# Weight combinations on VectorE in the gaps of tile 0, value copies in two halves, transposes one block later

## Chip, cores, metric

One core of a Trainium2 chip. The metric is the device time of one execution in microseconds (us), the median of several runs; before the change 313.4 us (lowest 312.9, highest 314.9). A "span" is the time from the first to the last instruction in a trace; it is some 1.7 us shorter than the device time of the same run.

## The reference, cut to what matters

```python
# attention: q, k, v of (batch 8, heads 8, seq 576, head_dim 64), window 32
scores = (q @ k.T) / 8                        # only where |i - j| <= 32
attn   = softmax(scores)                      # per row
x      = (attn @ v)  as  (4608 tokens, 512)
# feed-forward: w_in (512, 2048), w_out (2048, 512)
out    = gelu_tanh(x @ w_in) @ w_out          # float32 out
```

## The kernel before

The feed-forward runs over nine tiles (0 to 8) of 512 tokens. While TensorE multiplies tile t with `w_out`, the attention of batch t+1 is woven in between. From tile 1 on the second product is a Winograd-like scheme with 7 products in place of 8, which needs sums of activations (S1..S4, made per tile on VectorE) and combinations of weights made once: T1 = B12 - B11, T2 = B22 - T1, T3 = B22 - B12, T4 = B21 - T2, each 128 x 2048 in fp16 from quarters B of `w_out`.

For batch 2 and later, q and k are cast to fp16 on VectorE and transposed by DMA (`QT`, `KT`); the scores of tile t need `KT` of batch t+1. The values go straight into `V` by DMA from GpSimd's queue, and `pair_v` copies half of them to other partitions.

```python
PLAN_0 = {0: "s1@1 w0 w1", 4: "m0 m1", 12: "w2", ..., 52: "v2@0 v3@1",   # what is done at which step of tile 0
          56: "x2 t4", 57: "c1", 60: "x3", 64: "s4@1 m4"}                # s scores, m mask, v weigh, x spread,
...                                                                      # w cast w_out, t tails, c combine
def combine(i, eng):
    dst, x, y = wino["todo"][i]
    eng.tensor_tensor(dst, x, y, op=ALU.subtract)
...
                elif kind == "c":            # step 57 of tile 0
                    combine_w()
                    combine(1, nc.gpsimd)    # T1
...
        if t == 0:                           # after tile 0's last step
            for t4, yo in later:
                store(0, t4, yo)
            combine(2, nc.gpsimd)            # T2
            load_table(gelu_set)
...
def cast_and_turn(b):                        # first thing of tile 1 on VectorE (cut)
    queries(qr, q16, 0, 128)                 # 4 casts of q, then the DMA transpose QT<-q
    for pr in range(NPAIR):
        nc.vector.tensor_copy(k16[:, pr, :, :, :], kr[:, :, 2 * pr:2 * pr + 2, :])
        if pr % 2:
            nc.sync.dma_start_transpose(KT ... <- k16 of pairs pr - 1 and pr)
...
            for fc in range(begun, NF):      # input product of tile 1
                ffn_in(t, fc)
                if t == 1 and fc in (8, 12):
                    combine(fc // 4 + 1, nc.vector)          # T3, T4
                if t == 1 and fc == 3:
                    nc.gpsimd.tensor_copy(after, gTs[1][:, column(1, 2), 0:1])   # wait for the third gelu
                    load_v(2)                                # values of batch 2, from GpSimd's queue
...
            if t == 1 and i == 20:           # behind the masks m0 and m1 of step 16
                pair_v(unpaired.pop(0), nc.vector.tensor_copy)
```

The softmax here doesn't subtract the row's maximum and nothing guards it: scores larger than these inputs give would overflow.

Of the kernel before, what the change touches and what calls it, by code (L numbers as in the profile page):

```python
# [10 lines left out]
FP16 = mybir.dt.float16  # L11
# [25 lines left out]
def cut(b):  # L37
# [11 lines left out]



TURN_0 = {11: 0, 12: 1, 14: 2, 15: 3}
PLAN_0 = {0: "s1@1 w0 w1", 4: "m0 m1", 12: "w2", 18: "s2@0 s-1@1 m-1", 22: "d0", 24: "m2 d1",
          28: "s3@0 v-1@1 x-1", 30: "w3", 31: "m3", 34: "d2", 36: "v0@0 v1@1 x0 d3 x1", 52: "v2@0 v3@1",
          56: "x2 t4", 57: "c1", 60: "x3", 64: "s4@1 m4"}

ORDER_0 = [(t4, 4 * w + i) for w in range(4) for t4 in range(4)
           for i in ((2, 3, 0, 1) if w == 0 else range(4))]
# [6 lines left out]
def kernel(  # L65
# [9 lines left out]
    nc = tc.nc  # L75
# [25 lines left out]
    stage = ctx.enter_context(tc.tile_pool(name="stage", bufs=5))  # L101
# [19 lines left out]
    w_out16 = big.tile([128, NF, DM], FP16, name="w_out16")  # L121
# [50 lines left out]
    def load_v(b):  # L172
        V = Vs[b % 2]
        for c in range(4):
            nc.gpsimd.dma_start(V[:, c, :, :],  # L175
                                v[b, :, 128 * c:128 * c + 128, :].rearrange("h p d -> p h d"))
        nc.gpsimd.dma_start(V[0:64, 7, :, :], v[b, :, 512:S, :].rearrange("h p d -> p h d"))  # L177

    def pair_v(b, copy, hs=slice(0, H)):

        V = Vs[b % 2]
        copy(V[64:128, 4:8, hs, :], V[64:128, 0:4, hs, :])
        copy(V[0:64, 4:7, hs, :], V[0:64, 1:4, hs, :])  # L183
# [4 lines left out]
    def stage_w():  # L188
        return stage.tile([128, 4, 512], FP32, name="wst", tag="stage")
# [5 lines left out]
    def load_w_out(i, w, c0=0, c1=4):  # L195
        nc.sync.dma_start(w[:, c0:c1, :], w_out_v[:, 4 * i + c0:4 * i + c1, :])
        return w

    def cast_w(w, dst, on_dve=2, cs=range(4), on_act=()):
        for c in cs:  # L200
            (nc.scalar.copy if c in on_act else nc.vector.tensor_copy if c < on_dve else nc.gpsimd.tensor_copy)(  # L201
                dst[:, c, :], w[:, c, :])
# [59 lines left out]
    def cast_early(b, pr, engs):  # L262
        for src, dst, eng in zip(raws[b][0:2], halfs[b][0:2], engs):
            eng.tensor_copy(dst[:, pr, :, :, :].rearrange("p j h d -> p h j d"),
                            src[:, 2 * pr:2 * pr + 2, :].rearrange("p h (j d) -> p h j d", j=4))
# [24 lines left out]
    def trans_pair(b, pr, pt, now=True):  # L290
        q16, k16 = halfs[b][0:2]
        for j in range(4):
            nc.tensor.transpose(pt[:, j, :], q16[:, pr, j, :, :], idn)
        for j in range(4):
            nc.tensor.transpose(pt[:, 4 + j, :], k16[:, pr, j, :, :], idn)
        if now:
            trans_out(b, pr, pt)
# [134 lines left out]
    def column(t, n):  # L432

        return n // 2 + 8 * (n % 2) if t else n
# [27 lines left out]
    def gelu(t, n):  # L462
        fc = column(t, n)
        nc.scalar.activation(gTs[t][:, fc, :], phs[fc], AF.Gelu_apprx_tanh)  # L464
        if t and n % 4 == 3:
            sums(t, n // 4)

    wino = {}

    def combine_w():  # L470

        t12 = stage.tile([128, 2, 8, 256], FP16, name="t12", tag="stage")
        t34 = stage.tile([128, 2, 8, 256], FP16, name="t34", tag="stage")
        B11, B12, B21, B22 = (w_out16[:, r:r + 8, c:c + 256] for r in (0, 8) for c in (0, 256))
        T1, T2, T3, T4 = t12[:, 0], t12[:, 1], t34[:, 0], t34[:, 1]
        s12 = stage.tile([128, 2, 8, 256], FP16, name="s12", tag="stage")
        s34 = stage.tile([128, 2, 8, 256], FP16, name="s34", tag="stage")
        yo = stage.tile([128, 4, 512], FP32, name="y4", tag="stage")
        wino.update(B11=B11, B21=B21, B22=B22, T1=T1, T2=T2, T3=T3, T4=T4, S1=s12[:, 0],
                    S2=s12[:, 1], S3=s34[:, 0], S4=s34[:, 1], yo=yo,  # L480
                    todo={1: (T1, B12, B11), 2: (T2, B22, T1), 3: (T3, B22, B12), 4: (T4, B21, T2)})

    def combine(i, eng):
        dst, x, y = wino["todo"][i]
        eng.tensor_tensor(dst, x, y, op=ALU.subtract)  # L485
# [29 lines left out]
    later, unpaired = [], []  # L515
# [97 lines left out]
    wo = [load_w_out(0, stage_w())]  # L613
# [73 lines left out]
    split = (nc.gpsimd, nc.vector)  # L687
    cast_early(1, 0, split)
    cast_early(1, 1, split)
    for fc in range(6, NF):  # L690
        if fc in (11, 12):
            cast_early(1, fc - 9, split)
        if fc in TURN_0:
            pr = TURN_0[fc]
            if pr < 2:
                pt = psS.tile([128, 2, 8, 128], FP16, name="pt", tag=f"S{pr}")
            trans_pair(1, pr, pt[:, pr // 2] if pr < 3 else
                       psO.tile([128, 8, 128], FP16, name="pt", tag="O"))
        ffn_in(0, fc)
# [5 lines left out]
    for t in range(NT):  # L705
        b = t + 1
        att = b < B
        if t:
            for fc in range(begun):
                ffn_in(t, fc, 3, 4, then=False)  # L710
            for fc in range(begun):
                gelu(t, fc)
            if att and b > 1:
                cast_and_turn(b)
            for fc in range(begun, NF):
                ffn_in(t, fc)
                if t == 1 and fc in (8, 12):
                    combine(fc // 4 + 1, nc.vector)
                if t == 1 and fc == 3:

                    nc.gpsimd.tensor_copy(after, gTs[1][:, column(1, 2), 0:1])
                    load_v(2)
                    unpaired.append(2)
        plan = PLAN_0 if not t else PLAN if att else {5: "v-1", 31: "x-1"} if t == B - 1 else {}

        def group(g):
            return (b, g) if g >= 0 else (b - 1, 4)

        if plan and t:
            load_table(exp_set)  # L730
        if t and b + 1 < B:
            load_qk(b + 1)
        ods = {}
        for i in range(113 if t else 65):
            for act in plan.get(i, "").split():
                kind, at = act[0], int(act[act.index("@") + 1:]) if "@" in act else None
                g = int(act[1:].split("@")[0])
                if kind == "w":
                    if g == 3:
                        cast_v(1, 2)  # L740
                    cast_w(wo[g], w_out16[:, 4 * g:4 * g + 4, :], on_act=(1,) if g else ())
                    if g == 2:
                        cast_v(1, 0)
                        cast_v(1, 1)
                    if g == 3:
                        cast_v(1, 3)
                        cast_vt(1)
                        cast_tails(1, nc.gpsimd)
                        load_qk(2)
                elif kind == "t":  # L750
                    trans_tails(1, bank16(1))
                elif kind == "c":
                    combine_w()
                    combine(1, nc.gpsimd)
                elif kind == "s":
                    score(*group(g), at)
                elif kind == "d":
                    pair_v(b, nc.vector.tensor_copy, slice(2 * g, 2 * g + 2))
                elif kind == "m":
                    mask(*group(g))  # L760
                elif kind == "v":
                    bb, gg = group(g)
                    o, d = weigh(bb, gg, at)
                    ods[g] = (o, invert(bb, gg, o, d))
                    if t and g < 0 and b + 1 < B:
                        load_v(b + 1)
                        unpaired.append(b + 1)
                    if t and g == (3 if att else -1):
                        load_table(gelu_set)
                else:  # L770
                    spread(*group(g), *ods[g])
            if t == 1 and i == 20:
                pair_v(unpaired.pop(0), nc.vector.tensor_copy)
            if t == 0 and i in (61, 62):
                store(0, *later.pop(0), eng=nc.scalar)
            if t == 0 and i < 64:
                ffn_out_0(*ORDER_0[i])
            elif t and i < 112:
                ffn_out(t, i)
        if t == 0:  # L780
            for t4, yo in later:
                store(0, t4, yo)
            combine(2, nc.gpsimd)
            load_table(gelu_set)
        else:
            ffn_last(t)
        if unpaired:
            pair_v(unpaired.pop(), nc.sync.dma_start)
        begun = 3 if t < NT - 1 else 0
        for fc in range(begun):  # L790
            ffn_in(t + 1, fc, 0, 3)
# [28 lines left out]
```

## Time and profile before

| | before | what it says |
|---|---|---|
| time, median of runs | 313.4 us | the yardstick |
| the run whose trace was given | 310.07 us, span 308.4 us | faster than each of the timed runs of its session; this will matter |
| start of tile 1 (first L456 matmul after tile 0) | 58.9 us | tile 0 and the first attention |
| tile 1 | 39.4 us | the later tiles take 30.4 us |
| start of tile 2 to the end | 210.1 us | the same in every kernel below but one |

The last row makes the reading simple: span = start of tile 1 + length of tile 1 + 210.1. The lines that this comes from stand in the prediction.

### The profile page before, as it was taken

Reading aid. Unit: us, or ns where it says so; the run is one execution under the profiler, and the core shown is the slowest. Engines: PE = TensorE matmul, PEld = TensorE weight load, DVE = VectorE, ACT = ScalarE, POOL = GpSimd, SP = SyncE. Lnnn points to the kernel's source line nnn. Section 1 sums busy time; section 2 is a strip of 40 time slices with the busy share of each in tenths; the row PEclk is TensorE's granted clock in tenths of the full one; section 3 lists DMA queues with packets and bytes.
Section 4 is the critical chain, followed back from the end, with each engine's and each line's share of the span. In section 5 each row is a group of like instructions: output and inputs, shape, how many; then the busy total and the mean of one; then the engine's idle time right before and its main releaser. Section 6 shows DMA issues by size and latency. Waiting matters only on the chain.

```text
span 308.4 us, 7131 instructions
## 1 busy us (share of the span) xinstructions
PE 289.0 (94%) x2886; PEld 181.2 (59%) x2886; DVE 195.8 (63%) x425; ACT 186.9 (61%) x287; POOL 112.7 (37%) x162
## 2 busy tenths in 40 slices
PE   6989799895789999999999999999999999999993
PEld 2534444442567468746874686468646864784582
DVE  4783559799467846775677577666866644533451
ACT  1567385675355787478747874787478757705600
POOL 3666454896003910390049004800530051016000
PEclk9999999999699999999999999999999999999999
DMA  6999999979995999799979996999592022004013
GB/s 197 256 362 369 376 278 257 244 150 153 158 249 131 175 155 248 177 161 131 255 170 201 182 236 153 186 173 227 128 206 40 2 62 76 3 0 136 2 41 97
DMA packets 116831, 52.44 MB, mean 170 GB/s; under 512 B 97519, under 2 KB 109551, under 8 KB 116798
## 3 DMA queue, kind: packets, MB, share of 16 engines
q1 hardware_dynamic: 84233, 39.66, 59.2%
q0 software_dynamic: 31776, 11.41, 31.3%
q10 hardware_dynamic: 789, 0.92, 0.9%
q8 instruction: 22, 0.36, 0.5%
q14 instruction: 11, 0.09, 0.1%
HBM read 36.70 MB, written 9.44 MB: 150 GB/s over the span
## 4 chain that ended last, share of the span: by engine, by line
PE 77%; DMA 11%; SPq 5%; DVE 3%; POOL 1%; issue 1%; ACT 0%; DVEq 0%
PE mm L547 31%; PE mm L456 18%; PE ph L456 14%; DMA wst<-in_moe_w_in_dram 4%; PE ps_s L360 3%; DMA KT<-k 3%; PE ps_d L389 2%; DMA kr<-in_k_dram 2%; PE mm L521 2%; PE ps_o L395 2%; DMA kt<-in_k_dram 2%; SPq L145 2%; PE py L521 2%; SPq L136 1%; POOL t L485 1%
## 5 line engine op out<-in xcount | busy, mean ns | idle before, releaser
L456 PEld LDWEIGHTS <-w_in 128*128 128x128 f16 x576 | 56.0, 98 | 66.4 <-POOL w_in L201 1.4
L511 POOL DMA_DIRECT2D out_dram<-y x77 | 46.4, 610 | 114.6 <-DVE y L576 100.9
L456 PE MATMUL mm<-xT,w_in 128*128 128x512 f16 x320 | 78.6, 379 | 0.9 <-POOL w_in L201 0.7
L464 ACT ACTIVATE gT<-mm 128x512 f16<-128x512 f32 x80 | 47.6, 599 | 46.4 <-PE mm L456 45.6
L456 PE MATMUL ph<-xT,w_in 128*128 128x512 f16 x256 | 64.1, 379 | 0.0
L495 DVE TENSOR_TENSOR s<-gT 128x512 f16<-128x512 f16 x64 | 26.8, 419 | 41.7 <-ACT gT L464 41.7
L547 PEld LDWEIGHTS <-s 128*128 128x128 f16 x512 | 49.7, 98 | 6.0
L370 ACT ACTIVATE pe<-ps_s 128x960 f16<-128x960 f32 (+1 forms) x32 | 30.5, 976 | 30.6 <-PE ps_s L360 30.6
L547 PE MATMUL mm<-t,s 128*128 128x256 f16 x376 | 44.7, 273 | 0.0
L464 ACT ACTIVATE gT<-ph 128x512 f16<-128x512 f32 x64 | 36.0, 602 | 10.1 <-PE ph L456 9.9
L547 PEld LDWEIGHTS <-gT 128*128 128x128 f16 x384 | 36.6, 99 | 7.1
L547 PE MATMUL mm<-w_out,gT 128*128 128x256 f16 x256 | 34.0, 280 | 0.0
L409 ACT ACTIVATE lt<-lt 128x480 f32<-128x480 f32 (+3 forms) x40 | 23.5, 587 | 1.3
L175 POOL DMA_DIRECT2D V<-in_v_dram x24 | 22.2, 945 | 0.8 <-PE mm L456 0.8
L90 ACT ACT_TABLE_LOAD x17 | 21.8, 1283 | 1.1 <-PEq L804 0.8
L376 DVE TENSOR_TENSOR pe<-pe,band 128x960 f16<-128x960 f16 (+1 forms) x32 | 20.7, 662 | 2.5 <-ACT pe L370 2.5
L408 ACT ACTIVATE lt<-ps_d 128x480 f32<-128x480 f32 (+2 forms) x29 | 16.1, 554 | 10.0 <-PE ps_d L389 6.2
L360 PE MATMUL ps_s<-QT,KT 64*64 64x128 f16 (+3 forms) x576 | 13.6, 221 | 6.3 <-DMA KT<-k 5.6
L395 PEld LDWEIGHTS <-V 128*64 128x64 f16 x520 | 14.5, 112 | 5.9 <-DVE V L183 2.8
L360 PEld LDWEIGHTS <-KT 64*64 64x64 f16 x576 | 10.0, 109 | 13.2 <-DMA KT<-k 6.1
L547 PE MATMUL mm<-t,gT 128*128 128x256 f16 x128 | 16.3, 273 | 0.0
L177 POOL DMA_DIRECT2D V<-in_v_dram x6 | 4.6, 772 | 28.2 <-PE ps_o L395 28.2
(92 smaller groups left out, 324.2 us busy)
## 6 DMA issues: line engine op xcount, KB each, us to landing
kr<-in_k_dram SPq DMA_DIRECT2D x32, 256.0 KB, 8.2
qr<-in_q_dram SPq DMA_DIRECT2D x6, 1024.0 KB, 8.2
wst<-in_moe_w_in_dram SPq DMA_DIRECT2D x3, 1024.0 KB
wst<-in_moe_w_out_dram SPq DMA_DIRECT2D x3, 1024.0 KB, 11.9
V<-in_v_dram POOLq DMA_DIRECT2D x24, 128.0 KB, 8.0
qr<-in_q_dram SPq DMA_DIRECT2D x8, 256.0 KB, 10.7
vr<-in_v_dram SPq DMA_DIRECT2D x16, 128.0 KB, 4.1
V<-V SPq DMA_DIRECT2D x5, 256.0 KB
```

Of the source, the lines that this page charges most:

```text
L90: nc.scalar.add_instruction(mybir.InstLoadActFuncSet(name=nc.get_next_instruction_name(), act_func_set_id=which, ins=[], outs=[]))
L175: nc.gpsimd.dma_start(V[:, c, :, :], v[b, :, 128 * c:128 * c + 128, :].rearrange("h p d -> p h d"))
L360: nc.tensor.matmul(ps[64 * half:64 * half + 64, h, 4 * n * r:4 * n * r + 4 * n].rearrange("k (j p) -> k j p", j=4)[:, :, p0 - q0:p1 - q0], ...
L370: nc.scalar.activation(pe, ps[:, :, 0:w], AF.Exp, scale=SCALE)
L376: nc.vector.tensor_tensor(pe, pe, m.rearrange("k (o j) p -> k o j p", o=1).broadcast_to(list(pe.shape)), op=ALU.mult)
L395: nc.tensor.matmul(o[64 * h:64 * h + 64, cols].rearrange("d (j p) -> d j p", j=4)[:, :, p0 - q0:p1 - q0], Vs[b % 2][:, slot, 2 * pr + h, : ...
L409: nc.scalar.activation(lt[:, 0:n], lt[:, 0:n], AF.Exp, scale=-1.0)
L456: nc.tensor.matmul(ph, w_in16[:, dc, fc * 128:fc * 128 + 128], xT[:, dc, t * 512 % RING:t * 512 % RING + 512], start=(dc == 0), stop=(dc = ...
L464: nc.scalar.activation(gTs[t][:, fc, :], phs[fc], AF.Gelu_apprx_tanh)
L495: nc.vector.tensor_tensor(dst, x, y, op=op)
L511: (eng or turn_about[0] if t == NT - 1 else eng or nc.gpsimd).dma_start(out_v[b, j, q0 + p:q0 + p + e, cols], yo[m:m + e, cols])
L547: nc.tensor.matmul(pys["apart"][:, 0:256] if apart else py[:, blk, :], lhsT, wino[w][:, f, :], start=(new and i % (8 if one else 16) == 0) ...
```

## The change

The intent: take the two combinations T1 and T2 from GpSimd (4.06 and 4.07 us in the trace before) and put them on VectorE, where T3 and T4 take 1.22 us each in that trace, into gaps in which VectorE waited; copy the values of batch 2 in two halves, the first ahead of the masks; transpose batch 1 one block later, so that key casts don't stand ahead of the copies out of PSUM (the buffers in which the kernel puts TensorE's products).

```diff
--- before.py
+++ after.py
@@ -49,10 +49,10 @@
 
 
 
-TURN_0 = {11: 0, 12: 1, 14: 2, 15: 3}
-PLAN_0 = {0: "s1@1 w0 w1", 4: "m0 m1", 12: "w2", 18: "s2@0 s-1@1 m-1", 22: "d0", 24: "m2 d1",
-          28: "s3@0 v-1@1 x-1", 30: "w3", 31: "m3", 34: "d2", 36: "v0@0 v1@1 x0 d3 x1", 52: "v2@0 v3@1",
-          56: "x2 t4", 57: "c1", 60: "x3", 64: "s4@1 m4"}
+TURN_0 = {12: 0, 13: 1, 14: 2, 15: 3}
+PLAN_0 = {0: "s1@1 w1", 4: "m0 m1", 12: "w2", 17: "c1", 18: "s2@0 s-1@1 m-1", 22: "d0", 24: "m2 d1",
+          28: "s3@0 v-1@1 x-1", 30: "w3", 31: "m3", 34: "d2", 36: "v0@0 v1@1 x0 d3 x1", 52: "v2@0 v3@1 c2",
+          56: "x2", 60: "x3 t4", 64: "s4@1 m4"}
 
 ORDER_0 = [(t4, 4 * w + i) for w in range(4) for t4 in range(4)
            for i in ((2, 3, 0, 1) if w == 0 else range(4))]
@@ -468,17 +468,21 @@
     wino = {}
 
     def combine_w():
-
         t12 = stage.tile([128, 2, 8, 256], FP16, name="t12", tag="stage")
+        B11, B12, B21, B22 = (w_out16[:, r:r + 8, c:c + 256] for r in (0, 8) for c in (0, 256))
+        wino.update(B11=B11, B21=B21, B22=B22, T1=t12[:, 0], T2=t12[:, 1],
+                    todo={1: (t12[:, 0], B12, B11), 2: (t12[:, 1], B22, t12[:, 0])})
+        return B12
+
+    def wino_rest(B12):
         t34 = stage.tile([128, 2, 8, 256], FP16, name="t34", tag="stage")
-        B11, B12, B21, B22 = (w_out16[:, r:r + 8, c:c + 256] for r in (0, 8) for c in (0, 256))
-        T1, T2, T3, T4 = t12[:, 0], t12[:, 1], t34[:, 0], t34[:, 1]
+        T3, T4 = t34[:, 0], t34[:, 1]
         s12 = stage.tile([128, 2, 8, 256], FP16, name="s12", tag="stage")
         s34 = stage.tile([128, 2, 8, 256], FP16, name="s34", tag="stage")
         yo = stage.tile([128, 4, 512], FP32, name="y4", tag="stage")
-        wino.update(B11=B11, B21=B21, B22=B22, T1=T1, T2=T2, T3=T3, T4=T4, S1=s12[:, 0],
+        wino.update(T3=T3, T4=T4, S1=s12[:, 0],
                     S2=s12[:, 1], S3=s34[:, 0], S4=s34[:, 1], yo=yo,
-                    todo={1: (T1, B12, B11), 2: (T2, B22, T1), 3: (T3, B22, B12), 4: (T4, B21, T2)})
+                    todo=wino["todo"] | {3: (T3, wino["B22"], B12), 4: (T4, wino["B21"], wino["T2"])})
 
     def combine(i, eng):
         dst, x, y = wino["todo"][i]
@@ -688,10 +692,12 @@
     cast_early(1, 0, split)
     cast_early(1, 1, split)
     for fc in range(6, NF):
-        if fc in (11, 12):
-            cast_early(1, fc - 9, split)
         if fc in TURN_0:
             pr = TURN_0[fc]
+            if pr in (1, 2):
+                cast_early(1, pr + 1, split)
+            if pr == 3:
+                cast_w(wo[0], w_out16[:, 0:4, :])
             if pr < 2:
                 pt = psS.tile([128, 2, 8, 128], FP16, name="pt", tag=f"S{pr}")
             trans_pair(1, pr, pt[:, pr // 2] if pr < 3 else
@@ -750,8 +756,9 @@
                 elif kind == "t":
                     trans_tails(1, bank16(1))
                 elif kind == "c":
-                    combine_w()
-                    combine(1, nc.gpsimd)
+                    if g == 1:
+                        B12 = combine_w()
+                    combine(g, nc.vector)
                 elif kind == "s":
                     score(*group(g), at)
                 elif kind == "d":
@@ -769,8 +776,9 @@
                         load_table(gelu_set)
                 else:
                     spread(*group(g), *ods[g])
-            if t == 1 and i == 20:
-                pair_v(unpaired.pop(0), nc.vector.tensor_copy)
+            if t == 1 and i in (0, 40):
+                pair_v(2, nc.vector.tensor_copy, slice(i // 10, i // 10 + 4))
+                unpaired[:] = [3]
             if t == 0 and i in (61, 62):
                 store(0, *later.pop(0), eng=nc.scalar)
             if t == 0 and i < 64:
@@ -780,7 +788,7 @@
         if t == 0:
             for t4, yo in later:
                 store(0, t4, yo)
-            combine(2, nc.gpsimd)
+            wino_rest(B12)
             load_table(gelu_set)
         else:
             ffn_last(t)
```

## The prediction

"The lock", in it and below, is a name for what the trace before shows: a VectorE operation beside GpSimd's weight combination of 4.07 us ended just after it (a q cast took 4.79 us, 0.415 us in the median of its group). By what means was not tested.

> **What bounds the kernel now.** I first cut the span into tiles with the view of busy time by windows; the edges are the starts of the feed-forward input matmuls (L456) of each tile, taken from the chain that ended last. Columns: window, its length, then busy time of each engine, granted TensorE clock, DMA share, GB/s.
>
> ```profile
> 58.90:98.30 39.40, 32.69 (x343) 21.17 (x332) 30.48 (x55) 23.76 (x35) 15.87 (x16) 0.91 1.25 175
> 98.46:128.87 30.41, 30.41 (x331) 20.01 (x330) 20.89 (x47) 21.55 (x33) 11.39 (x17) 1.00 1.22 187
> 128.87:159.29 30.42, 30.42 (x332) 20.05 (x330) 20.89 (x47) 21.55 (x33) 11.33 (x17) 1.00 1.24 178
> ```
>
> From tile 2 on TensorE is busy all the time and a tile takes 30.4 us; the change touches nothing there. Tile 1 does nearly the same matmuls and takes 98.46 - 58.93 = 39.5 us: **9.1 us too many**. Its clock is also the only one of these at 0.91. That stretch is the prize[...].
>
> Then the chain of waits from tile 0's end into tile 1 (start, length, what held it):
>
> ```profile
> 54.82 4.07 POOL t L485
> ...
> 59.03 5.55 DMA kt<-in_k_dram
> ...
> 65.55 0.75 DVE q L321 x2
> 66.30 2.07 DVE k L329 x4
> 68.37 1.86 DVE qt L321 x4
> 70.23 8.67 DMA KT<-k
> ...
> 78.94 1.01 PE ps_s L360 x30
> ...
> 85.70 0.69 DVE V L182
> 86.40 0.56 DVE V L183
> ```
>
> Tile 1 runs into a wait for the transposed keys of batch 2 (KT), which come through casts on VectorE and DMA transposes, and later into the value copies (L182, L183). The list of waits, filtered for TensorE, gives the sizes:
>
> ```profile
> PE ps_s L360 <- DMA KT<-k: 5.6, 1, 5.6
> PE pt L293 <- DVE KT L301: 1.3, 1, 1.3
> ...
> PE ps_od L395 <- DVE V L183: 1.1, 1, 1.1
> ...
> PE pt L285 <- DVE yo L527: 0.8, 1, 0.8
> ```
>
> The timeline says why KT is late. The casts of q come at 60.41, but:
>
> ```profile
> 60.84 4.79 DVE L321 CAST q<-qr 128x512 f16<-128x512 f32 x1
> 61.27 4.07 POOL L485 TENSOR_TENSOR t<-w_out,t 128x2048 f16<-128x2048 f16 x1
> ```
>
> One cast, 0.415 us in the median of its group, took 4.79 us, and it ends just after GpSimd's 4.07 us weight combination. The two overlap almost exactly: a stand-still of 4.79 - 0.42 = 4.4 us.
>
> Finally the clock, in one-microsecond windows: 1.00 until 76, 0.65 from 76 to 77, 0.50 from 77 to 83, 0.94 from 83 to 84. TensorE went idle at 73.35, so the clock fell after about 3 us of idleness and came back about 4.1 us after work resumed. In those 4.1 us 128x256 matmuls are spaced 2.61 / 12 = 0.217 us, against 3.27 / 29 = 0.113 us later. So about 2.1 us are lost. Check: 5.6 (KT) + 2.1 (clock) + 1.3 (values; 1.1 in the list, 1.4 on the weight-load side) = 9.0 of the 9.1 us.
>
> [...]
>
> **The change part by part.**
>
> *Combination T2 (and T1) from GpSimd to VectorE.* Removed: 2 x 4.06 us on GpSimd, at 54.82 and 61.27. Added: 2 x 1.22 us on VectorE. T1 (step 17) falls into the idle time of 1.37 us before the tail's mask at 45.93; T2 (step 52) into that of 1.19 us before the copy at 55.85. The first gap has GpSimd's casts in it (43.41 to 45.58), so it may stretch by 0.5 us; VectorE is busy 3.90 of 4 us from 46 to 50, so such a delay passes on. After T2 moves, the four q casts take 4 x 0.415 = 1.7 us from about 60.2, so they end near 61.9 in place of 66.3. The DMA transpose of Q is issued near 62 (66.37 before). The loads of k, qt and kt land only by 64.58 (59.03 + 5.55), so k's casts probably wait until about 63.3 (my estimate: the kt load was last in its queue). Two of them, 0.83 us, give 64.2. Q's issue took 3.77 us, so the first K transpose is issued near 65.7 (70.23 before): 4.5 us earlier. With the same 8.67 us, KT lands at 74.4. TensorE reaches the scores near 73.1. **Idle 5.6 becomes about 1.3: -4.3 us.** An idle of 1.3 us did not lower the clock at 35.2, so **-2.1 us** more.
>
> *Value copies in halves.* The 0.69 + 0.55 us before the weighing at 87.01 are replaced by half as much ahead of the masks. TensorE's wait of 1.3 us goes, if the values have landed. Their loads move from 65.62 to about 63.4 (they wait for the third gelu, then GpSimd is free). The fourth is issued near 67; landings run from 4.5 to 10.9 us, so 71.5 to 78. VectorE reaches the first half near 75. If it stands there until 78, masks come late and part of the wait returns: I count **-1.0**.
>
> *Transposes one block later, w0's cast earlier.* The third pair's transposes waited 1.3 us because VectorE held the copies of the second pair behind key casts that waited for DMA. The casts now come after the first pair's copies: locally about -1.1 us. But tile 0 then meets data that comes when it comes: the last value pair lands at 51.9 and x1 ends at 54.06, just before the weighing that needs its bank (54.24). So nearly all of this is taken back. The tail transposes (t4), four steps later, avoid their 0.8 us wait, but T2 now delays the copy of that bank to about 56.6, and the last scores need x3 and the tail copies, near 58.4 instead of 58.63. **-0.3 us** for both.
>
> Sum: 4.3 + 2.1 + 1.0 + 0.3 = 7.7. Since three of the terms can only shrink I take 7.4: 313.68 - 7.4 = **306.3 us**.
>
> **The rivals.** (a) *A DMA bound in place of the lock.* The Q transpose stands behind k's loads in the same queue until 64.6, and the DMA share is 1.9 to 2.0 from 70 to 78. If transposes get going only at 64.6, the 12.5 us from the first Q issue (66.37) to KT (78.9) give 77.1: idle 4.0, clock lost again, and a gain of only 1.5 + 1.0 + 0.3 = 2.8 us (310.9). For it: the queue's order. Against: part of those 12.5 us is Q's issue, which goes on during the loads, and in tiles 2 to 6 KT arrives some 11 us after Q's first issue. I give it 1 in 5. (b) *The values' landing blocks VectorE* ahead of the masks: the 1.3 us stay or grow by 1 us; 307.5 or so. For: landings up to 10.9 us; against: TensorE needs masks only at step 33. (c) *Tile 0 gets longer*, since VectorE is nearly full from 46 to 54: T1 behind GpSimd's casts costs up to 0.5 us; 307. (d) *Everything hides:* no idle at all before the scores and tile 1 at 30.4: gain 9.1 + 0.3, so 304.3.
>
> **Range and chances.** Between (d) at 304.3 and a mix of (b), (c) and a late KT at 309.5 lies most of it; (a) in full is outside. Two per cent is 6.3 us, or 307.4. The base case and (d) clear it, (a) doesn't, (b) and (c) come near it: faster 0.72, same 0.26, slower 0.02; slower would take a new wait larger than the 5.6 us, of which I see no sign.
>
> **What would show it right or wrong.** No GpSimd row L485; four VectorE rows of about 1.22 us; the longest q cast near 0.45 us; the wait of scores for KT at 0 to 2 us; clock 1.00 in tile 1; no wait of L395 for L183 at step 33; tile 1 about 31.5 us instead of 39.5; tile 0's end at 58 to 59. It is wrong if KT lands after 76, if the clock still falls, or if casts of q stand waiting for their load instead of the lock.

## The result, and the profile after

304.1 us in the first session (303.85 to 305.38, 4 runs) against 313.4 us: ratio 0.9704, 95% interval 0.966 to 0.975. A ratio is the mean time of one kernel's fast runs over the mean of the other's fast runs of the same rounds, so not quite the ratio of the medians quoted. Two more sessions on other occasions gave 0.9713 and 0.9764. The time lies 0.2 us below the predicted range of 304.3 to 309.5; the lock was as told, a landing time was not, and the gain was larger: 9.3 us in place of 7.4. (The prediction started from 313.68 us, the median of three runs; the fourth made it 313.4.)

Tile 1 after, by the view of busy time in windows (window, length, busy time of PE, PEld, DVE, ACT, POOL, granted clock, DMA share, GB/s):

```profile
60.69:92.31 31.62, 31.01 (x339) 20.13 (x331) 25.78 (x57) 23.64 (x35) 11.44 (x15) 1.00 1.49 219
```

31.6 us in place of 39.4, at full clock, with 0.6 us idle. (The prediction had said "about 31.5"; its own terms, 39.5 - 4.3 - 2.1 - 1.0, give 32.1.) But the tile starts at 60.7, later than the 58.9 of the trace before. The list of waits of TensorE, with the lines that answer to those of before:

```profile
PE mm L551 <- DVE y L562: 0.5, 1, 0.5
...
PE ps_s L360 <- DVE QT L287: 0.4, 1, 0.4
...
PE pt L293 <- DVE KT L301: 0.2, 1, 0.2
```

The waits for `KT` (5.6) and for the value copies (1.1) are gone; a new one of 0.5 us is for a copy out of PSUM that now stands behind the first half of the value copies, and one of 0.4 us, at the end of tile 0, is for the tails that are transposed later. The wait for L301 went from 1.3 to 0.2, and that for the copy of `yo` (0.8) vanished too.

The timeline of the changed kernel from the casts to the scores (start, length, engine, line):

```profile
62.13 1.43 DVE L321 CAST q<-qr 128x512 f16<-128x512 f32 x4
63.62 3.90 SPq L324 DMA_TRANSPOSE QT<-q  x1
65.24 4.04 POOL L175 DMA_DIRECT2D V<-in_v_dram  x4 [0.35 <-POOL after L727]
65.78 1.97 DVE L329 CAST k<-kr 128x512 f16<-128x512 f32 x4 [2.22 <-DMA kr<-in_k_dram]
67.61 4.25 SPq L331 DMA_TRANSPOSE KT<-k  x2
75.04 0.62 PE L360 MATMUL ps_s<-QT,KT 64*64 64x96 f16 x32
```

Four q casts take 1.43 us, not 5.89. The k casts wait for their load, as predicted. The scores start at 75.04 without a wait for `KT`. The view of DMA issues (last number: us from issue to landing, here of the first of the two `KT` transposes, for which the scores wait) has

```profile
KT<-k SPq DMA_TRANSPOSE x1, 6.0
```

so `KT` landed at 73.6, 6.0 us after its issue at 67.61, not 8.67 (6.5 and 6.9 in the two other sessions' traces). And one more thing has turned round: the Q transpose is now issued 1.6 us ahead of the first value load. Before, the value loads came first:

```profile
65.62 4.28 POOL L175 DMA_DIRECT2D V<-in_v_dram  x4
66.37 3.77 SPq L324 DMA_TRANSPOSE QT<-q  x1
```

### The profile page after: what moved, and what is told of

Same layout as the page of the kernel before. It is cut to its first block, busy times and chain, and to the rows that moved or that the text cites. A ratio compares the mean times of both kernels' runs of the same rounds, so it can differ in the third digit from the quotient of the medians.

```text
span 302.4 us, 7135 instructions
## 1 busy us (share of the span) xinstructions
PE 289.4 (96%) x2886; PEld 181.3 (60%) x2886; DVE 195.0 (64%) x429; ACT 186.9 (62%) x287; POOL 104.6 (35%) x160
## 4 chain that ended last, share of the span: by engine, by line
PE 71%; DMA 11%; SPq 8%; DVE 5%; POOL 2%; issue 2%; ACT 0%; DVEq 0%; POOLq 0%
PE mm L551 31%; PE mm L456 18%; PE ph L456 14%; DMA wst<-in_moe_w_in_dram 4%; DMA wst<-in_moe_w_out_dram 3%; SPq L145 3%; PE ps_s L360 2%; PE ps_d L389 2%; DMA kr<-in_k_dram 2%; DMA vr<-in_v_dram 2%; SPq L136 2%; DVE s L499 2%; PE ps_o L395 2%; SPq L167 2%; POOL w_in L201 1%
## 5 line engine op out<-in xcount | busy, mean ns | idle before, releaser
L456 PE MATMUL ph<-xT,w_in 128*128 128x512 f16 x256 | 65.0, 383 | 0.0
L370 ACT ACTIVATE pe<-ps_s 128x960 f16<-128x960 f32 (+1 forms) x32 | 30.5, 976 | 22.5 <-PE ps_s L360 22.4
L551 PE MATMUL mm<-w_out,gT 128*128 128x256 f16 x256 | 32.8, 273 | 0.5 <-DVE y L562 0.5
L175 POOL DMA_DIRECT2D V<-in_v_dram x24 | 22.0, 938 | 1.7 <-PE mm L456 1.3
L418 DVE TENSOR_TENSOR xT<-ps_o,lt 128x480 f16<-128x480 f32 (+5 forms) x26 | 13.4, 535 | 2.0 <-ACT lt L409 1.9
L551 PE MATMUL mm<-w_out,s 128*128 128x256 f16 x120 | 14.4, 273 | 0.0
```

The lines of the kernel that those rows point to most:

```text
L175: nc.gpsimd.dma_start(V[:, c, :, :], v[b, :, 128 * c:128 * c + 128, :].rearrange("h p d -> p h d"))
L370: nc.scalar.activation(pe, ps[:, :, 0:w], AF.Exp, scale=SCALE)
L456: nc.tensor.matmul(ph, w_in16[:, dc, fc * 128:fc * 128 + 128], xT[:, dc, t * 512 % RING:t * 512 % RING + 512], start=(dc == 0), stop=(dc = ...
L551: nc.tensor.matmul(pys["apart"][:, 0:256] if apart else py[:, blk, :], lhsT, wino[w][:, f, :], start=(new and i % (8 if one else 16) == 0) ...
```

## The experiments

All are timed in rounds with the kernel before on the same chip. T stands for the start of tile 1 in the trace in question. "Fast" excludes runs over 1.5% above the fastest of their kernel, which are named where they matter. No build was refused.

| run | ratio (95%) | T, us | tile 1, us | wait for KT |
|---|---|---|---|---|
| before, given trace | | 58.9 | 39.4 | 5.6 |
| before, again | 1.000 (0.996 to 1.005) | 61.5 | 40.2 | 6.4 |
| change, first trace | 0.970 (0.966 to 0.975) | 60.7 | 31.6 | 0 |
| change, second session | 0.971 (0.967 to 0.976) | 59.4 | 31.6 | 0 |
| change, third session | 0.976 (0.973 to 0.979) | 60.0 | 31.6 | 0 |
| only combinations | 0.970 (0.966 to 0.974) | slow run | | |
| only combinations, again | 0.973 (0.968 to 0.978) | 62.7 | 31.9 | 0 |
| only value halves | 0.995 (0.990 to 0.999) | 60.2 | 39.2 | 6.9 |
| only later transposes | 0.994 (0.990 to 0.999) | 59.3 | 42.5 | 8.7 |
| change without halves | 0.976 (0.971 to 0.981) | 60.5 | 34.8 | 0.6 |
| change without later transposes | 0.971 (0.968 to 0.975) | 60.9 | 30.5 | 0 |
| change + useless GpSimd op, T2's place | 0.996 (0.992 to 1.001) | 59.5 | 37.6 | 5.2 |
| change + useless GpSimd op, T1's place | 0.973 (0.968 to 0.978) | 58.3 | 36.0 | 3.8 |
| before + 20 matmuls in the wait | 0.998 (0.994 to 1.002) | 59.4 | 40.0 | (2.4) |
| before + 28 matmuls in the wait | 0.997 (0.993 to 1.000) | 60.0 | 38.7 | (0.8) |
| T2 on VectorE, not in the gap | 0.988 (0.983 to 0.992) | 59.8 | 37.8 | 3.9 |
| same, value loads held back | 0.979 (0.974 to 0.984) | 60.5 | 34.3 | 0 |
| before, value loads held back | 0.989 (0.985 to 0.994) | 61.2 | 36.7 | 3.2 |
| change, T3 and T4 ahead | 0.972 (0.968 to 0.976) | 59.3 | 30.5 | 0, then 1.6 in tile 2 |
| change, value loads held back a little | 0.971 (0.969 to 0.974) | 60.2 | 32.1 | 0 |

In brackets: what was left of the wait after the useless matmuls. T runs from 58.3 to 62.7 us with no order by kernel (its mean is 60.1 us over the nine traces with T1 on GpSimd, and 60.1 over the other eleven). What sets it was not tested; the lists show waits for weights ahead of it in every trace. One trace is therefore no measure of it.

### The kernel before, again

No edit.

> The kernel before, unchanged, against itself. Ratio 1.000. It is there for its profile: the one that the prediction was worked from belongs to a run of 310.07 us, while the timed runs of the same kernel have a median of 313.4. Theory A (the mechanism was right, the prediction subtracted a gain from the wrong run): a profile of a usual run shows about 3 us more than the first one, either ahead of tile 1 (weights landing later, as they did in the trace of the changed kernel, where tile 1 starts at 60.7 in place of 58.9) or in the wait of the scores for KT (above 5.6 us). Rival B (the timed runs are slow for a reason that no trace shows): the profile looks as before, near 308.4 us span.

Measured: 313.33 us median (310.18 to 313.94), ratio 1.0001. The profiled run is a usual one, 313.41 us, span 311.7:

```profile
61.45:101.61 40.16, 32.60 (x338) 21.14 (x331) 30.52 (x55) 23.74 (x35) 16.18 (x17) 0.92 1.24 169
```

and its list of waits and timeline:

```profile
PE ps_s L360 <- DMA KT<-k: 6.4, 1, 6.4
```

```profile
62.51 4.94 DVE L376 TENSOR_TENSOR pet<-pet,band 128x768 f16<-128x768 f16 x1 [0.56 <-ACT pet L370]
62.95 4.07 POOL L485 TENSOR_TENSOR t<-w_out,t 128x2048 f16<-128x2048 f16 x1
67.37 1.79 DVE L321 CAST q<-qr 128x512 f16<-128x512 f32 x4
```

Theory A holds, on both counts: 2.5 us later into tile 1, 0.8 us more wait for `KT`. Here it is not a cast that stands still beside T2, but the mask ahead of it (0.56 us in the given trace, 4.94 here). In each of the two traces the VectorE operation that met the 4.07 us operation paid for it (4.79 and 4.94 us), and the casts after it came late.

### Each part alone

Only combinations: the plan gets `17: "c1"` and `52: "... c2"`, `combine(g, nc.vector)`, all else as before. Only halves: `if t == 1 and i in (0, 40): pair_v(2, ..., slice(i // 10, i // 10 + 4))`. Only later transposes: `TURN_0 = {12: 0, 13: 1, 14: 2, 15: 3}` with the casts moved, `t4` at step 60.

Theory A of the first is that the stand-still beside T2 and the lowered clock after it are the main thing.

> The kernel before with only the two weight combinations T1 and T2 moved to VectorE in the gaps. Theory A [...]: ratio about 0.978, 7 us less, KT waited for 0 to 1 us, clock 1.00 in tile 1, the wait for the value copies of 1.1 us still there. Rival C (the three parts share the gain about equally): 0.990 or more.

> The kernel before with only the value copies of batch 2 in two halves. Theory A: the wait of 1.1 to 1.4 us at step 33 of tile 1 goes, KT and clock stay as they are: 1.0 to 1.3 us less, ratio about 0.996. Rival C: 3 us less, 0.990. Rival D (the first half stands in front of the masks until the values land): no gain, 1.000.

> The kernel before with only the later transposes of batch 1, the earlier cast of the first w_out block and the tails' transposes four steps later. Theory A: tile 0 meets landing data, and q's cast stands behind T2 anyway: 0 to 0.5 us, ratio 0.999. Rival C: 2 to 3 us less, 0.992.

Measured: combinations 303.56 us, ratio 0.9702, as much as the whole change; halves 311.42 us, 0.9948; transposes 311.31 us, 0.9944. The parts don't add up to the whole, and rival C falls. The combinations gave more than the 7 us expected. Halves did about what was expected (1.6 us, interval 0.2 to 3.0). The transposes gave 1.7 us in the mean, more than the 0 to 0.5 expected, but the interval reaches down to 0.4. Its trace can't name a source: it belongs to the slowest of the six runs (313.65 us), in which T2 began late (T + 3.6), `KT` was waited for 8.7 us and the clock was halved for some 10 us (an estimate from its mean clock of 0.984 over 311.9 us). So that stays open. The profiled run of the combinations was their one slow run (307.51 us), so it is not compared. For what it is worth, from tile 2 on it takes 210.1 us like the others; its tile 1 takes 35.5 us, with waits of 1.2 us for `KT` and 1.7 for the values and half the clock for 3.4 us.

### Each part undone

> The changed kernel, unchanged, on the chip of the next three, as their yardstick: ratio 0.970 to the kernel before, tile 1 at 31.6 us, no wait for KT.

> The changed kernel with the value copies of batch 2 whole again, behind the masks. The combination part alone had given 0.970, as much as the whole change. Theory F (once KT is on time the value wait is back at step 33 and the halves take it away): 1.0 to 1.7 us more than the changed kernel, ratio to before about 0.974, with a wait for L183 of 1.1 to 1.7 us in the trace. Rival G (the halves only shift VectorE's work, and the wait for the masks takes the place of the one for the values): the same as the changed kernel within 0.4 us.

> The changed kernel with the transposes of batch 1, the first w_out cast and the tails' transposes where they were. Theory F: 0.3 to 0.8 us more (the waits of 1.3 us for L301 and 0.8 us for the yo copy are back, most of it hidden by landing weights and values). Rival G: the same within 0.3 us, or even less time, since the first w_out cast then doesn't hold VectorE.

> The combination part alone once more, since its profile fell in an outlier of 307.5 us. Theory F: on the same chip it is 1.3 to 2.5 us slower than the changed kernel (ratio to before 0.975 to 0.978). Rival G: equal to the changed kernel, 0.970; the other two parts then add nothing to it. The profile should show KT without a wait and the wait for L183 still there.

On one chip: change 303.65 us (0.9713, with one slow run of 309.87), without halves 305.59 us (0.9761, one slow run of 309.33), without later transposes 303.29 us (0.9714, none slow), combinations alone 304.04 us (0.9731, one slow run of 307.41). The traces of the run without halves (307.08 us) and of the combinations alone (306.50) are those of their slowest fast runs. So:

- The later transposes add nothing once the combinations have moved: rival G. Their waits did shrink in the trace (L301 from 1.3 to 0.2); that the data that tile 0 meets next come no earlier, as the prediction argued, was not tested.
- The halves: 1.5 us in the mean of fast runs, intervals overlapping, so not clear by time. The trace of the run without them shows what they prevent:

```profile
PE ps_od L395 <- DVE V L183: 1.8, 1, 1.8
```

and in the windows of the same run, the clock (the number ahead of the last two):

```profile
81.00:82.00 1.00, 0.00 (x0) 0.00 (x0) 0.96 (x3) 0.23 (x1) 0.00 (x0) 1.00 1.53 198
82.00:83.00 1.00, 0.66 (x28) 0.57 (x28) 1.00 (x3) 0.24 (x1) 0.00 (x0) 1.00 1.34 274
83.00:84.00 1.00, 1.00 (x17) 0.79 (x12) 0.45 (x1) 0.97 (x3) 0.00 (x0) 0.79 1.34 274
84.00:86.00 2.00, 2.00 (x11) 1.44 (x10) 0.72 (x2) 1.03 (x2) 0.00 (x0) 0.50 1.24 303
86.00:87.00 1.00, 1.00 (x7) 0.70 (x5) 0.92 (x2) 0.00 (x0) 0.00 (x0) 0.51 1.34 261
```

Here the clock fell at about 83.6, after a wait of 1.8 us and when TensorE had been back at work for 1.2 us (from 82.34). Tile 1 took 34.8 us there. In the trace of the combinations alone, a wait of 1.2 us at the same place left the clock alone (the next 15 matmuls of 128x256 took 1.81 us, as in the given trace before at a clock of 1.00; tile 1 31.9 us). So in these two traces this wait cost its own length, and in one of them half the clock for 3.4 us on top.

How long the clock stayed down can be read from such windows (a window at 0.79 is 0.42 us at half clock): 0.42 + 2.00 + 0.98 = 3.4 us here. It is 3.4 us too in the first trace of the change (22.5 to 25.9, in tile 0), in that of the combinations' slow run and in that with 20 spins, and 6.8 us in the given trace before (76.3 to 83.1), in that of before, again, and in that with T2 on VectorE, not in the gap. What decides when it falls was not found: in the given trace before it fell about 3 us after TensorE had gone idle (73.35), here after a wait of 1.8 us and 1.2 us of work. A wait thus cost the clock in some traces and not in others.

### The lock, put back by itself

To the changed kernel, one operation whose result nobody reads is added where T2 stood:

```diff
             wino_rest(B12)
+            nc.gpsimd.tensor_tensor(wino["T3"], wino["B22"], B12, op=ALU.subtract)
```

> The changed kernel plus one tensor_tensor on GpSimd, of the same shape, just where T2 stood; its result is thrown away (the place is written again by T3 before it is read). Theory A (the lock between GpSimd's two-input operation and VectorE's casts): the q casts stand still until it ends, KT is late, TensorE idles and its clock falls: 5 to 8 us more, ratio to before 0.987 to 0.995. Rival H (what mattered was where T2's own result or the later value loads stood): the cast timing is as in the changed kernel and the time within 1 us of it, 0.970 to 0.974.

Measured: 310.04 us, ratio 0.9962 (all six runs between 308.4 and 312.7). Nearly the whole gain is given back by one operation that computes nothing needed. Its timeline:

```profile
60.41 4.67 DVE L376 TENSOR_TENSOR pet<-pet,band 128x768 f16<-128x768 f16 x1 [0.71 <-ACT pet L370]
60.59 4.08 POOL L792 TENSOR_TENSOR t<-w_out 128x2048 f16<-128x2048 f16 x1
65.01 1.79 DVE L321 CAST q<-qr 128x512 f16<-128x512 f32 x4
...
79.08 1.01 PE L360 MATMUL ps_s<-QT,KT 64*64 64x96 f16 x32 [5.21 <-DMA KT<-k]
```

The stand-still (4.67 us for the mask, 0.56 in the given trace before), the late `KT` (a wait of 5.2 us) and the lowered clock (0.985 in the mean, 0.994 in the first trace of the change) are all back. Rival H falls as far as T2's own result goes: the operation's being there is enough. But it also puts the first value load back ahead of the Q transpose (65.08 against 66.86), so this run does not tell the lock from the order of the transfers; the runs on `KT`'s landing below do.

The same operation at the place of T1 (a step `57: "e"` that issues it):

> The changed kernel with the same useless GpSimd operation as in the run that gave the time back, but at the place of T1 (step 57), where no VectorE operation on the way to KT follows at once. Theory A (it is the lock on the casts, not GpSimd's load as such): within 1 us of the changed kernel, ratio 0.970 to 0.974[...]. Rival: GpSimd work anywhere in tile 0 costs: 0.985 or more, and T1 had its share.

Measured: four fast runs at 302.3, 302.7, 303.5 and 306.2 us and two slow ones at 307.2 and 309.6; fast ratio 0.973. The mean of the fast runs lies within those of the change in its three sessions (0.970 to 0.976; the change itself was not timed on this chip), so theory A holds in the main. But it may not be free, with two slow runs of six: its trace (the run of 306.2 us) has the mask at 1.61 in place of 0.56 us, the Q transpose issued at 62.27, only 0.3 us ahead of the first value load, and a wait of 3.8 us for `KT`, which landed 9.8 us after its issue. Why 1 us should cost so much is the next question but one.

### The clock

Useless matmuls on TensorE where it waits for `KT`:

```diff
             for act in plan.get(i, "").split():
+            # ahead of it:  if t == 1 and i == 4: spin(20, 512)     (28 in the second run)
```

> The kernel before with 20 useless 128x512 matmuls (4.3 us) on TensorE where it would stand waiting for KT. The wait for KT ends when it did. Theory A (2.1 us of the excess of tile 1 is the lowered clock): clock 1.00 in tile 1, 1.8 to 2.4 us less than before, ratio 0.993, although TensorE has more to do. Rival (the clock costs nothing there because other waits bind): ratio 1.000.

> The kernel before with 28 useless matmuls (6.0 us) in the wait for KT. The run with 20 was too short: its trace has the spins over at 78.1, KT at 80.5 and the clock down from 80.3 to 83.3, so only 2.8 of the 4.1 us of slow work were left out of it and the gain was 0.7 us. If the clock is worth the 2 us of the prediction: clock 1.00 through tile 1, 1.5 to 2.4 us less than before, ratio 0.993 to 0.995. If it is not: 1.000.

Measured: 20 matmuls 310.51 us, ratio 0.9978; 28 matmuls 311.01 us, ratio 0.9968 (0.9934 to 1.0001), each near 1 us and neither clear of nothing. The first was a poor test: the spins ended at 78.1, the clock fell at 80.3, 2.2 us later, and `KT` came at 80.5. In the second the clock stayed at 1.00:

```profile
81.20 0.62 PE L360 MATMUL ps_s<-QT,KT 64*64 64x96 f16 x32 [0.76 <-DMA KT<-k]
```

From here to tile 2's start (98.65) are 17.4 us; in the trace of the kernel before, again, the same stretch takes 101.61 - 82.32 = 19.3 us, in the changed kernel 92.31 - 75.04 = 17.3. In the traces the clock is thus worth 1.8 us of the 2.1 predicted. In the timed runs 1.0 us is the mean, with anything from 0 to 2 us in the interval, although all six had a mean clock of 0.994 to 0.999 (before: 0.979 to 0.989). The 28 spins last some 6.0 us and would themselves outlast a wait of 5.6 us, so they may hide part of the gain. That the lowered clock costs time is shown by the traces, how much in timed runs only to that width.

### Why KT came sooner than 8.67 us after its issue

T2 alone is moved to VectorE, just ahead of the q casts where it had stood; T1 stays on GpSimd (`combine(2, nc.vector)` in place of `combine(2, nc.gpsimd)`). Then the same with the value loads of batch 2 held back, and the kernel before with only that:

```diff
-                if t == 1 and fc == 3:
-                    nc.gpsimd.tensor_copy(after, gTs[1][:, column(1, 2), 0:1])
+                if t == 1 and fc == 9:
+                    nc.gpsimd.tensor_copy(after, gTs[1][:, column(1, 8), 0:1])
```

> The kernel before with T2 alone moved to VectorE, and not into the gap but where it stood, just ahead of the q casts; T1 stays on GpSimd, nothing else of the change. Theory A: what cost was the 4 us lock on the q casts, so this has most of it: KT waited for 0 to 1 us, ratio 0.973 to 0.980 (it adds 1.2 us ahead of the casts, which then wait less for k's loads). Rival (T1 on GpSimd costs as much): 0.985 or more.

Theory J of the next two is that the transposes land late because value loads are in flight with them.

> The run with T2 on VectorE where it stood had KT issued as early as the changed kernel (67.6), but KT landed 10.6 us later, not in under 7.4. There the Q transpose was issued at the same moment as the first value load; in the changed kernel it is 1.6 us ahead of it. This is the same kernel with the value loads of batch 2 held back until the gelu of block 8. Theory J [...]: the wait for KT of 3.9 us goes to 0 to 1, ratio 0.972 to 0.978. Rival K (the 1.2 us of T2 ahead of the casts are the whole cause): wait still 3 to 4 us, 0.9875.

> The kernel before with the value loads held back likewise. Theory J: KT lands in some 7.3 us after its issue, not 8.7 to 9.2, the wait for KT falls from 5.6 to 6.4 to about 4.5, and the time by 1 to 2 us (0.994 to 0.997), unless the values then come too late for the weighing (wait for L183 above 2 us). Rival K: KT's wait stays at 5.6 to 6.4, ratio 1.000.

Measured: T2 late 307.03 us, ratio 0.9875, worse than expected; with the value loads held back 305.62 us, 0.979; before with value loads held back 308.66 us, 0.9893. The timeline of T2 late:

```profile
64.05 3.42 SPq L324 DMA_TRANSPOSE QT<-q  x1
64.10 3.98 POOL L175 DMA_DIRECT2D V<-in_v_dram  x4
...
67.56 6.26 SPq L331 DMA_TRANSPOSE KT<-k  x2
...
78.18 1.01 PE L360 MATMUL ps_s<-QT,KT 64*64 64x96 f16 x32 [3.93 <-DMA KT<-k]
```

and with the loads held back:

```profile
64.59 3.00 SPq L324 DMA_TRANSPOSE QT<-q  x1
67.69 2.62 SPq L331 DMA_TRANSPOSE KT<-k  x2
69.36 3.57 POOL L175 DMA_DIRECT2D V<-in_v_dram  x4
...
74.84 0.62 PE L360 MATMUL ps_s<-QT,KT 64*64 64x96 f16 x32
```

The view of DMA issues gives `KT`'s landing in the first and in the second:

```profile
KT<-k SPq DMA_TRANSPOSE x1, 10.6
...
KT<-k SPq DMA_TRANSPOSE x1, 3.2
```

`KT` is issued at the same time in both (67.6, 67.7), and lands 10.6 us later in one and 3.2 us later in the other. Only the value loads stand elsewhere. Theory J holds in this: the transposes lose to value loads that are in flight with them. By what means was not tested. All 20 traces fit: where the first value load was issued 3.5 to 5.8 us ahead of `KT`, it took 8.5 to 10.6 us to land, where 1.3 to 3.3 us ahead, 6.0 to 7.6. (The one exception is the next run.) The time isn't all back (0.979, not 0.970). Part of that is the whole value copies, as in the change without halves (0.976). Part is that the held-back values come late for their own use: VectorE waits 0.7 us for them, TensorE 1.9 us for L183, and the clock falls (0.989 in the mean of that run).

The kernel before shows a gain too, with the lock still in place: 3.4 us, more than the 1 to 2 expected. It is not the landing that gives most of it: `KT` took 8.2 us, not the 7.3 expected and 9.3 in the usual run, with the first value load at 70.05, still 0.55 us ahead of it. Part of it is on VectorE itself:

```profile
67.16 1.42 DVE L321 CAST q<-qr 128x512 f16<-128x512 f32 x4
68.50 1.42 DVE L329 CAST k<-kr 128x512 f16<-128x512 f32 x4
```

The casts take 1.42 and 1.42 us here, 1.79 and 2.14 in the usual run of before, where GpSimd issues value loads beside them. Q's issue takes 1.86 us and not 3.63, and `KT` is issued at T + 9.4 in place of T + 11.5.

So GpSimd's T2 did harm twice. It held the casts for 4 us, and as the value loads stood behind it in GpSimd's queue, they started at the very moment at which the casts were let go (65.62 and 65.63 in the given trace), and ahead of the Q transpose (66.37). With T2 gone the value loads wait for a gelu, the casts don't, and the transposes lead (by 1.6 us in the first trace of the change).

### Two versions that might be better

T3 and T4 moved into VectorE's wait for k's load:

```diff
         queries(qr, q16, 0, 128)
+        if b == 2:
+            combine(3, nc.vector)
+            combine(4, nc.vector)
```

> The changed kernel with T3 and T4 moved ahead, into VectorE's wait of 2.1 to 2.2 us for the loads of k (between the casts of q and those of k) in place of after blocks 8 and 12 of tile 1. If the chain of VectorE (casts, sums, T3, T4, masks) is what is left of tile 1's excess (31.6 us against 30.4), 0.5 to 1.1 us less than the changed kernel, ratio 0.968. If k's loads land early in most runs, T3 and T4 only delay the k casts: no gain or 1 us worse.

Measured: 302.71 us, ratio 0.9717, not the 0.968 hoped for; not better than the change. Tile 1 did come down to 30.5 us, the length of a later tile. (It is 30.5 us also in the trace without later transposes, where k's loads had landed in time and VectorE did not wait 2.2 us for them. It fits that this wait is what the change leaves of tile 1's excess.) But tile 2 rose from 30.4 to 32.2, and its list of waits has a new first line:

```profile
PE ps_s L363 <- DMA KT<-k: 1.6, 1, 1.6
```

It is the same wait for the keys, now of batch 3: those loads (kr issued from 73.3 to 86.6) had not moved ahead with TensorE.

The changed kernel with the value loads held back a little (`fc == 5`, block 4), beside the change itself:

> The changed kernel with the value loads of batch 2 held back until the gelu of block 4 instead of block 2 (some 1.5 us later). Theory J: transposes then always lead the value loads by 3 us, so the slow runs of the changed kernel (304.9 and 309.9 of six) become rarer and the median is 0.3 to 0.8 us lower; tile 1 at 30.5 to 31.6 us. If the values then land after VectorE has reached their copies (T + 17.5 us), masks wait and it is 0.5 to 2 us slower.

> The changed kernel once more as the yardstick on the same chip: 0.970 to 0.972 to before; for the spread of tile 1's start and of its length.

Measured: 304.13 us (303.0 to 304.6, 5 runs), ratio 0.9713 (0.9692 to 0.9735), against 305.40 us (303.4 to 308.9), 0.9764 (0.9733 to 0.9794). The Q transpose leads the value loads by 2.8 us there, and no run is slow; tile 1 took 32.1 us in its trace, over the 30.5 to 31.6 expected, with a wait of 1.0 us for L562. It fits a race between transposes and loads as the source of the change's slower runs (306.9 and 308.9 here, 309.9 in the second session), but no slow run of the change was profiled, and the two intervals just touch. What is on record of those three runs is their mean clock, 0.987, against 0.991 to 1.000 in the other runs of the change. It is a candidate, not a shown improvement.

## Why the prediction was off, step by step

- **"Tile 1 ... 9.1 us too many. That stretch is the prize": right** (9.0 by the edges 58.90 and 98.30 of its own first line). From tile 2 to the end every trace has 210.1 us, but for the one with T3 and T4 ahead.
- **The lock: right.** The stand-still of 4.4 us was there, and the useless operation brings it back, with the late value order (0.9962). That it could hold the mask in place of a cast was not seen, and makes no difference to the sum.
- **"With the same 8.67 us, KT lands at 74.4 ... Idle 5.6 becomes about 1.3: -4.3 us": this is the step that failed.** The issue came as worked out (T + 6.8 predicted, T + 6.9 measured), the landing did not. The measured term is about -6.4: from 6.4 us in the usual run that was traced to none. It was short at both ends. 8.67 us was a landing beside value loads that had started first; in the changed kernel the transposes lead, and `KT` took 6.0 us: it landed at T + 12.9, not T + 15.5, ahead of TensorE at T + 14.35, and the 1.3 us of idle did not come. The given trace had a warning: the one other landing of `KT` that its view of DMA issues gives, in tile 5, is 6.7 us. And 5.6 us was the wait of a lucky run, 310.07 us in a session with a median of 313.4; the usual run waits 6.4. I took the gain from the one and subtracted it from the median of the others.
- **Rival (a), a DMA bound, was taken the wrong way round.** I asked if k's loads would block the transposes; what was in flight with them to their harm were the value loads (`KT` landed after 10.6 us beside them, after 3.2 without), and the change moved those behind. The prediction had the new start of the value loads right (T + 4.5; measured T + 4.55), and that of the Q transpose (T + 3.1; T + 2.9), and used the first only for the values' own landing.
- **Clock -2.1 and values -1.0: -2.0 together.** From the scores to tile 2 the trace shrank from 19.3 to 17.3 us. The clock alone gives 1.8 of it in the trace with 28 spins. The wait for values (1.1) went, but 0.5 us for L562 came; what the halves also took away is the lowered clock of the trace without them (3.4 us at half). So tile 1's 31.6 us against "about 31.5" is luck: the idle that was predicted and did not come is made up for by some 1.1 us that these two terms did not give.
- **-0.3 for the later transposes: too small to be seen**; undoing them in the changed kernel changes 0.0 (0.9714 against 0.9713).
- **The sum.** 4.3 + 2.1 + 1.0 + 0.3 = 7.7, cut to 7.4 as "three of the terms can only shrink". From the usual trace of before to that of after: 6.5 until the scores (T + 20.9 to T + 14.35) and 2.0 behind them make 8.5 of tile 1; the remaining 0.8 of 9.3 is the start of tile 1 (61.45 to 60.69), which is luck in these two traces (T has the same mean with T1 on GpSimd and without). Tile 0's end was predicted at 58 to 59 and was at 60.7. Over three sessions the change gives 7.4 to 9.3 us (0.9764 to 0.9704), so the cut was uncalled for: the first term grew.
- **Range.** Its low end was "no idle at all and tile 1 at 30.4", 304.3, reckoned from 313.68; from the first session's 313.4 it is 304.0. Tile 1 was at 31.6, and still the time was 304.1, because the gain was counted from the tile 1 of the lucky trace (39.4 us, not 40.2) and the start of tile 1 added its luck. That the time lies just outside is a matter of sessions: the third gave the predicted 7.4 us. That the first term was too small does not hang on it.

What stays open: the size of the clock's share in timed runs (0 to 2 us), why the later transposes alone gave 1.7 us on the kernel before, by what means value loads slow the transposes, what decides when the clock falls, and what the slow runs of the change are.

## What to carry to other kernels

Look for an operation whose one instance is ten times its group's median, and see which long operation of the neighbour engine lies exactly beside it; moving that neighbour was worth more here than the stand-still of 4.4 us (the combinations alone gave a ratio of 0.970, about 9 us), since it had also released the casts and the value loads late. Before taking over a landing time from a trace, look what else was in flight then, and whether the change reorders it. And a gain read from one trace belongs to that run: compare its time with the timed median first, and take a second trace if they differ by more than the effects that you are adding up.

## What was measured of the hardware

- While GpSimd issues value loads, four k casts on VectorE take 2.14 us (before, again), and 1.42 us when it doesn't (before, value loads held back); q casts 1.79 and 1.42. In the given trace before, four value loads took 4.28 us to issue beside these casts, and the next four 3.51 us after them.
- An fp16 subtraction of 128 x 2048 took 4.06 us on GpSimd and 1.22 on VectorE (the given trace before, L485), 3.3 times.
- The clock fell about 3 us after TensorE went idle (the given trace before), 2.2 us after the last matmul (20 spins), and after a wait of only 1.8 us, 1.2 us after work had resumed (without halves); a wait of 1.2 us was harmless once (combinations alone, again).
- `KT` landed 10.6 us after its issue beside value loads and 3.2 us without them.
